# Products for VectorE, another order of the groups' pattern, and the seventh group routed through TensorE in a fused attention and expert kernel

## The chip, the cores and the metric

The kernel runs on one core of a Trainium2 chip. The metric is the device time of one execution in microseconds (us), as the median of several runs. The engines are TensorE (PE for its matmuls, PEld for its weight loads), VectorE (DVE), ScalarE (ACT), GpSimd (POOL) and SyncE (SP); each works through its own queue of instructions in order, and semaphores order the queues among each other. DMA transfers are issued from the queues of SP, ACT and POOL.

## The reference

Three stages follow one another: gated linear attention, a dense gated product, and a routed mixture of experts.

```python
# q, k, v, alpha: (4, 8, 768, 48)
for t in range(S):
    state = alpha[:, :, t, :, None] * state + einsum('bhd,bhe->bhde', k[:, :, t], v[:, :, t])
    y[:, :, t] = einsum('bhd,bhde->bhe', q[:, :, t], state)
x = y, as 3072 tokens of 384
x = (x @ w_a) * (x @ w_b) @ w_out          # 384 -> 1536 -> 384
logits = x @ w_gate + modality_bias[modality_id]   # 8 experts
e_idx = argmax(logits); gate_w = softmax(logits)[e_idx]
out[token] = gate_w * (relu(x @ w1[e_idx]) @ w2[e_idx])   # 384 -> 1024 -> 384
```

## The kernel before

The 3072 tokens are cut into eight groups (w = 0 to 7) of 384 tokens, two groups to a batch of the attention. A group has three chunks (c = 0 to 2) of 128 tokens and twelve features (f = 0 to 11), each a slice of 128 columns of `w_a` and `w_b` and 128 rows of `w_out`. Float32 operands of the dense stage are split in a high and a low part, and each product is three passes, so one feature of one group is 18 matmuls into `ab` (token m, L723), which ScalarE copies (`asb`, L728), VectorE multiplies (`g`, token g, L734), ScalarE rounds (`gh`, L736), VectorE subtracts (`gl`, token l, L741), and nine matmuls into `px` (token p, L693). TensorE runs m of one feature before p of the one before it.

A chunk of the attention goes through these tokens. 1, 2 and 3 each take the next piece of `prepare`: transpose and clip alpha, the scan `R` (L419) with its reciprocals, the scaled keys `kt` (L428), and then the scan `at` (L430), the transpose of q and the product `qt` (L432). S are the scores of `qt` and `kt` on TensorE (L444). M masks them into `sm`. V is three steps in one: `pads` copies a part of v on ScalarE (L471), `decay` multiplies the running `state` by `R` (L477), and `values` makes the output `y` from `state` (L492, L504) and from `sm` (L508, L513) on TensorE. H rounds `y` to `xh` on ScalarE (L525), X subtracts to `xl` on VectorE (L529); T turns the keys (L535) and copies them to `ktok` (L537); U makes the update `u` (L543) and D adds it to `state` (L559, L561). A class attribute `early` marks groups 0 and 1; `LATE` is 3.

Before the change, `qt` is on VectorE for groups 0 to 2 and on GpSimd for groups 3 to 7, and `decay` is on VectorE for group 0 and on GpSimd after it. The mask of groups 0 to 2 is a copy on ScalarE (L461) and a select on GpSimd (L462); that of groups 3 to 7 is one product on VectorE (L464).

The routing of a group (`route`, token R for its next piece) has two forms. With gate columns, 24 products with a running sum on VectorE (`junk`, L771, each with an 81 ns read of its sum) give the logits of three tiles of 128 tokens, two products to a piece. Without them, TensorE transposes `xr` (L779), ScalarE copies it (`xT`, L781) and TensorE multiplies by `wg_sb` (L785). Both go on with the argmax on VectorE (to `oh`, L806), the rank on TensorE (L815 to L819), the positions on VectorE, and three scattered writes from GpSimd's queue, `tab_d<-rec,posi` (L832), here called the puts. The table `tab_d` is filled beforehand by `clear_table` (L1241), a memset and a DMA from GpSimd's queue. W makes the gate columns, Z loads inputs, i ids, r one piece of a weight's conversion, and Y checks late inputs.

The order of DVE, PE, SP and ACT is written out by hand in two lists: SEQ, for the products of groups 0 and 1 with the attention of groups 1 and 2, and STEADY, run five times (w = 2 to 6, each four lines a chunk), which interleaves the products of group w with the attention of group w + 1 and the routing of group w - 1. A line of STEADY is one feature. Group 0's attention comes first (`first`). Group 7's products, group 6's routing and the table of the first expert slots stand in a later part (pool `m2`): one feature, five features beside the routing, two more, and then the last four beside `slots[0].split()`, which converts the first expert's weights (`w0he` and so on, L1067) as they land (`w1re`). The landing of `w1re` hangs on the puts of the routing, since the table of rows `rte` is read after them (L1019) and the slot's loads follow it. After that the expert slots run.

Of the kernel before, what the change touches and what calls it, by code (L numbers as in the profile page):

```python
# [20 lines left out]
P = 128  # L21
# [10 lines left out]
SEQ = (  # L32
# [16 lines left out]
)  # L49
# [14 lines left out]
)  # L64
WARM0, WARM1 = 7, (0, 3, 4, 0, 3, 0, 0, 0, 1)
ORDER0 = 3, 0, 1, 2, 1
MIX = 5, 2, 3
SPLIT = 4
# [5 lines left out]
def gla_moe_kernel(ctx, tc, q, k, v, alpha, w_a, w_b, w_out, modality_id, w_gate, modality_bias, w1, w2, out):  # L74
# [162 lines left out]
    def load_ids():  # L237
        idr = ap.tile([P, H * D], I32, tag="v", bufs=4, name="idr")[:NT, : 2 * P]
        nc.sync.dma_start(out=idr, in_=modality_id.rearrange("(t p) -> t p", p=P).bitcast(I32))
        mb = const.tile([P, 2, E], F32, name="mb")  # L240
        nc.sync.dma_start(out=mb, in_=modality_bias.rearrange("(o m) e -> o m e", o=1).broadcast_to([P, 2, E]))
        yield
        idf = ap.tile([NT, P], F32, tag="sm", bufs=3, name="idf")
# [11 lines left out]
        t0 = ap.tile([P, NT, E], F32, tag="sm", bufs=3, name="bias0")  # L255
# [67 lines left out]
    class Attention:  # L323
# [79 lines left out]
        def prepare(self, c):  # L403
# [27 lines left out]
            q0, qt = self.turned("q", c, 2)  # L431
            (nc.vector if self.w < LATE else nc.gpsimd).tensor_tensor(qt, q0, at, op=ALU.mult)  # L432
            self.ready[c] = Rp[:, :, 1:2], kt, qt
# [14 lines left out]
        def mask(self, c):  # L448
            self.sc[c] = []
            for g, pt in enumerate(self.pts.pop(c)):  # L450
# [8 lines left out]
                pv = pt.rearrange("p (h t) -> p h t", h=NPAIR)  # L459
                if self.w < LATE:  # L460
                    nc.scalar.activation(sm, pv, AF.Copy)  # L461
# [11 lines left out]
        def decay(self, c):  # L473

            if self.gc(c):
                R = self.ready[c][0]
                (nc.gpsimd if self.w else nc.vector).tensor_tensor(  # L477
                    state, state, R.broadcast_to([P, NPAIR, 2 * D]), op=ALU.mult
                )

        def values(self, c):
# [7 lines left out]
            if later:  # L489
                for kk in range(2):  # L490
                    for i in range(2):
                        mm = nc.tensor.matmul(  # L492
                            py[64 * i : 64 * i + 64, kk, :], state[:, 2 * kk + i, :64], qt[:, 2 * kk + i, :], start=(kk == 0), stop=False
                        )
                        if not (kk or i or self.w < LATE):
                            for n in ("mask", "pads"):
# [164 lines left out]
    def tokens(*groups):  # L661
# [14 lines left out]
        p = chain.from_iterable(a.prepare(c) for a in groups for c in range(CPW))  # L676
        names = dict(S=["scores"], M=["mask"], V=["pads", "decay", "values"], H=["high"], X=["low"], T=["keys"], U=["carry"], D=["add"])
        return {**{nm.upper(): turns(nm) for nm in "akq"}, **dict.fromkeys("123", p), **{t: each(*does) for t, does in names.items()}}

    def lazily(make):  # L680
        yield from make()

# [65 lines left out]
    def moe(w):  # L748
        for piece in products([(w, f) for f in range(NF)]):
            if piece in "le":  # L750
                yield

# [11 lines left out]
    def route(w, pool, puts, gate=None):  # L764
# [3 lines left out]
        for t in range(CPW):  # L768
# [7 lines left out]
            else:  # L776
                pt = ptile(f"xT{w}_{t}")
                for kk in range(KD):
                    nc.tensor.transpose(pt[:, kk * P : (kk + 1) * P], xr[w][t][:, kk * P : (kk + 1) * P], ident)  # L779
                xt = pool.tile([P, 512], F32, tag="sm", bufs=3, name=f"xT{w}_{t}")[:, :DM]  # L780
                nc.scalar.activation(xt, pt[:, :DM], AF.Copy)  # L781
# [458 lines left out]
    def clear_table():  # L1240
        fill = ap.tile([P, TAB // P * 2], F32, tag="sm", bufs=3, name="fill")  # L1241
        nc.gpsimd.memset(fill, BIG)
        nc.gpsimd.dma_start(out=tab_d.rearrange("(p r) c -> p (r c)", p=P), in_=fill)

    def turn_gate():

        pt = ptile("gateT")
        for kk in range(KD):
            nc.tensor.matmul(pt[:E, kk * P : (kk + 1) * P], wg_sb[:, kk, :], ident, start=True, stop=True)
        t = ap.tile([P, 512], F32, tag="sm", bufs=3, name="gateT")[:E, :DM]  # L1250
        nc.scalar.activation(t, pt[:E, :DM], AF.Copy)
        nc.scalar.dma_start(out=wgt_d[:, :], in_=t)

    def pipeline(y_d=None):
# [3 lines left out]
        with tc.tile_pool(name="att", bufs=1) as ap:  # L1258
# [19 lines left out]
            if y_d is None:  # L1278
                with tc.manual_schedule(engines={EN.DVE, EN.PE, EN.SP, EN.Activation}):
# [7 lines left out]
                    def second():  # L1287
# [4 lines left out]
                        load_weights(1, "ab")  # L1292
                        clear_table()

# [3 lines left out]
                    def gate_turn():  # L1298
                        turn_gate()
                        gate.append(gate_columns("gate", ap, 2, tag="cv", bufs=4))  # L1300
                        yield
# [19 lines left out]

                    extra = {"r": rest, "i": load_ids(), "W": gate_turn(), "Z": chain(then_load(then), then_load(nxt)), "R": lazily(lambda: route(0, ap, puts))}
                    todo = halves + [(w, f) for w in range(2, NW - 1) for f in range(NF)]
                    joint = products(todo)
# [29 lines left out]
                    for w in range(2, NW - 1):  # L1354
# [3 lines left out]
                        emit(STEADY, {**groups[w + 1], **kinds, "0": groups[w + 2]["1"]})  # L1358
                        assert not any(True for _ in chain(*(groups[w + 1][c] for c in "1SMVHXTUD"), *kinds.values()))
                    assert next(rest, None) is None  # L1360
                    assert next(joint) == "e"
            else:
# [10 lines left out]
        with tc.tile_pool(name="m2", bufs=2) as m2:  # L1373
            fold = small("fold", [P, TINY])
            nc.vector.tensor_reduce(fold, ident.rearrange("p (j c) -> p c j", c=TINY), axis=AX.X, op=ALU.add)
            last = moe(NW - 1)
            gate = gate_columns("last", m2, 4, tag="wr", bufs=6) if y_d is None else None
            run((islice(last, 1), 1))
            early = []
            run((islice(last, MIX[0]), 1), (behind(chain(route(NW - 2, m2, puts, gate), early_table(early))), 2))  # L1380
            slots = [Slot(f"e{i}", "e", i, 2, (NW - 1) * WIN) for i in range(NEARLY)]
# [173 lines left out]
```

## Time and profile before

| | us |
|---|---|
| median of 3 runs | 867.98 |
| lowest and highest of them | 867.70, 869.49 |
| the profiled execution, whole | 876.44 |
| its span, first to last instruction | 874.6 |
| busy: PE, DVE, ACT, POOL | 819.8, 674.0, 292.7, 206.0 |
| mean granted clock of TensorE | 0.987 |

The profiled execution is 8.46 us longer than the median of the runs, and 1.84 us longer than its own span. Rows of the trace give times from the span's start.

### The profile page before, as it was taken

The numbers are of one execution on the slowest core, as the hardware profiler recorded it, in microseconds if no ns is written. First come the engines' busy times: TensorE is split into PE (matmuls) and PEld (weight loads), VectorE is DVE, ScalarE is ACT, GpSimd is POOL, SyncE is SP. The second block draws the span as 40 slices with busy tenths as digits, with TensorE's granted clock in tenths as the row PEclk, the third lists the DMA queues.
The fourth block names the chain that finished last, engine by engine and source line by source line (L and its number), as shares of the span: only waits on it lengthen the run. The fifth ranks groups of instructions, "written<-read, shape, count | busy, mean of one in ns | idle before, by whom it ended". The sixth has DMA issues, their size and how long they took to land.

```text
span 874.6 us, 16828 instructions
## 1 busy us (share of the span) xinstructions
PE 819.8 (94%) x6193; PEld 771.2 (88%) x6193; DVE 674.0 (77%) x1495; ACT 292.7 (33%) x684; POOL 206.0 (24%) x283
## 2 busy tenths in 40 slices
PE   7778999999999998999999999899799999999995
PEld 6667998988998998998899899899699998998994
DVE  7878898659887987998998888774569876675641
ACT  2233442331222222221222222121555565564640
POOL 5221100102111012111111111102426554555421
PEclk9899999999999999999999999999899999999998
DMA  9988842716412410422422220030943988695900
GB/s 170 195 191 201 209 123 73 195 52 81 110 28 63 107 50 2 136 56 54 118 64 64 62 59 1 2 100 2 385 130 137 326 313 275 184 362 162 314 33 23
DMA packets 127089, 113.93 MB, mean 130 GB/s; under 512 B 55919, under 2 KB 105875, under 8 KB 126996
## 3 DMA queue, kind: packets, MB, share of 16 engines
q1 hardware_dynamic: 116260, 100.57, 42.2%
q0 software_dynamic: 4480, 10.99, 3.6%
q10 hardware_dynamic: 6256, 1.19, 1.1%
q8 instruction: 51, 0.84, 0.5%
q14 instruction: 42, 0.34, 0.1%
HBM read 101.87 MB, written 11.00 MB: 129 GB/s over the span
## 4 chain that ended last, share of the span: by engine, by line
PE 61%; DVE 21%; issue 6%; ACT 3%; POOL 3%; DMA 2%; another core or an unknown queue 2%; SPq 1%; DVEq 0%; POOLq 0%; ACTq 0%
PE ab L723 19%; PE px L693 9%; PE hl L1155 9%; PE pol L1103 8%; DVE R L419 3%; DVE at L430 2%; DVE g L734 2%; PE he L1155 2%; PE poe L1103 2%; PE s L444 2%; PE u L543 2%; DVE junk L771 2%; DVE kt L397 2%; DVE qt L397 1%
## 5 line engine op out<-in xcount | busy, mean ns | idle before, releaser
L723 PE MATMUL ab<-xh,pa 128*128 128x384 f32 x576 | 166.0, 342 | 7.9 <-ACT asb L728 5.5
L723 PE MATMUL ab<-xh,pb 128*128 128x384 f32 x576 | 163.4, 337 | 3.5 <-DVE pb L225 2.8
L693 PE MATMUL px<-po,gh 128*128 128x384 f32 x576 | 148.3, 342 | 0.4 <-DVE po L225 0.4
L723 PEld LDWEIGHTS ab<-xh,pa 128*128 128x128 f32 x576 | 106.4, 189 | 9.6 <-ACT asb L728 5.8
L723 PEld LDWEIGHTS ab<-xh,pb 128*128 128x128 f32 x576 | 106.1, 189 | 5.4 <-DVE pb L225 3.7
L736 ACT ACTIVATE gh<-g 128x384 fp32r<-128x384 f32 x96 | 50.3, 524 | 172.7 <-DVE g L734 171.4
L693 PEld LDWEIGHTS px<-po,gh 128*128 128x128 f32 x576 | 101.8, 188 | 3.8 <-issue 1.0
L723 PE MATMUL ab<-xl,pa 128*128 128x384 f32 x288 | 97.2, 337 | 0.3
L723 PE MATMUL ab<-xl,pb 128*128 128x384 f32 x288 | 96.8, 336 | 0.0
L728 ACT ACTIVATE asb<-ab 128x384 f32<-128x384 f32 x96 | 46.9, 489 | 145.5 <-PE ab L723 143.5
L693 PE MATMUL px<-po,gl 128*128 128x384 f32 x288 | 94.4, 337 | 0.3 <-DVE gl L741 0.3
L734 DVE TENSOR_TENSOR g<-ab,asb 128x384 f32<-128x384 f32 x96 | 53.2, 554 | 50.6 <-issue 26.7
L1160 DVE SCALAR_TENSOR_TENSOR hll<-hl,hhl 128x256 fp32r<-128x256 f32 x72 | 30.3, 421 | 54.1 <-ACT hhl L1158 50.4
L771 DVE SCALAR_TENSOR_TENSOR junk<-xr,gate 128x384 bf16<-128x384 f32 x96 | 65.2, 679 | 2.4
L477 POOL TENSOR_TENSOR state<-state,R 128x384 f32<-128x384 f32 x18 | 16.1, 895 | 203.1 <-DVE R L419 193.9
L741 DVE TENSOR_TENSOR gl<-g,gh 128x384 fp32r<-128x384 f32 x96 | 54.0, 563 | 9.7 <-ACT gh L736 9.7
L723 PEld LDWEIGHTS ab<-xl,pa 128*128 128x128 f32 x288 | 54.6, 190 | 0.8 <-DVE xl L529 0.8
L693 PEld LDWEIGHTS px<-po,gl 128*128 128x128 f32 x288 | 53.8, 188 | 1.0 <-DVE gl L741 1.0
L723 PEld LDWEIGHTS ab<-xl,pb 128*128 128x128 f32 x288 | 54.5, 189 | 0.0
L1158 ACT ACTIVATE hhl<-hl 128x256 fp32r<-128x256 f32 x72 | 27.7, 384 | 63.4 <-PE hl L1155 55.0
L832 POOL DMA_INDIRECT tab_d<-rec,posi x24 | 24.2, 1009 | 89.7 <-DVE base L829 50.1
L432 POOL TENSOR_TENSOR qt<-qt,at 128x512 f32<-128x512 f32 x15 | 20.3, 1355 | 89.3 <-DVE qt L397 89.3
(340 smaller groups left out, 1871.4 us busy)
## 6 DMA issues: line engine op xcount, KB each, us to landing
w1rl<-in_moe_w SPq DMA_DIRECT2D x18, 768.0 KB
w2rl<-in_moe_w SPq DMA_DIRECT2D x18, 768.0 KB
raw_a<-in_alpha SPq DMA_DIRECT2D x72, 96.0 KB
raw_k<-in_k SPq DMA_DIRECT2D x72, 96.0 KB
raw_q<-in_q SPq DMA_DIRECT2D x72, 96.0 KB
wo<-in_moe_w_out SPq DMA_DIRECT2D x6, 768.0 KB
w1re<-in_moe_w SPq DMA_DIRECT2D x6, 768.0 KB
w2re<-in_moe_w SPq DMA_DIRECT2D x6, 768.0 KB
```

The source lines that it names most:

```text
L397: nc.vector.transpose(t.rearrange("p a (r n) -> p a n r", n=self.TPP), self.raws.pop((nm, c)).rearrange("p a (n d) -> p a n d", d=D)[:, :, ...
L693: newest["mm"] = nc.tensor.matmul(px[w][t][:, :DM], a_, b_, start=(first and i == 0), stop=(last and i == 2))
L723: nc.tensor.matmul(pt[:, :WIN], a_, b_, start=(i == 0), stop=(i == 3 * KD - 1))
L728: nc.scalar.activation(asb, pt[:, :WIN], AF.Copy)
L734: nc.vector.tensor_tensor(g, pab[1][:, :WIN], asb, op=ALU.mult)
L736: newest["act"] = nc.scalar.activation(gh, g, AF.Copy)
L741: newest["gl"] = nc.vector.tensor_tensor(gl, g, gh, op=ALU.subtract)
L771: nc.vector.scalar_tensor_tensor(junk, xr[w][t], 1.0, gate[e], op0=ALU.mult, op1=ALU.mult, accum_out=L[:, t, e : e + 1])
L1103: newest["mm"] = nc.tensor.matmul(self.po[t][:, :DM], a_, b_, start=(f == 0 and i == 0), stop=(f == NF2 - 1 and i == 2))
L1155: nc.tensor.matmul(pt[:, :n], a_, b_, start=(i == 0), stop=(i == 3 * KD - 1))
L1158: nc.scalar.activation(gh[:, :n], pt[:, :n], AF.Relu)
L1160: nc.vector.scalar_tensor_tensor(gl[:, :n], pt[:, :n], 0.0, gh[:, :n], op0=ALU.max, op1=ALU.subtract)
```

## The change

The change has seven parts (paths with `y_d` given are not run). (a) `qt` and `decay` are on VectorE for all groups. (b) Group 2's mask is made on VectorE too, and the dependence of `values` on the mask and the pads holds from group 2 on. (c) `decay` and `pads` become a token of their own, E, which stands before M; V keeps only `values`; T stands before V; the next group's token 0 stands behind l. (d) In STEADY the sixth and twelfth pieces of the routing stand one line earlier or later than before, the rank (piece 14) one feature after the argmax (piece 13), and the last piece (positions and puts) behind D at the end. (e) `clear_table` leaves the start and becomes token C beside feature work of groups 0 and 1; `gate_turn` gives two pieces, the second at the end of SEQ. (f) Small tiles change their pool's tag from `sm` (3 buffers) to `cv` (4 buffers). (g) Group 7's first four features are interleaved with group 6's routing in a new list, FINAL, and that routing has no gate columns; the later part continues with one, two and then the remaining features, with `MIX = 1, 2, 2`.

```diff
-    "m p g 2 l i"
+    "m p g 2 l i C"
...
-    "m S W p g M l 1"
-    "m V H T p U g 2 X l D"
...
+    "m S W p g E M l 1"
+    "m T V H p U g 2 X l D"
...
 STEADY = (
     "m p g 1 l 2"
     "m p g 3 l R R"
-    "m S p g R l M R R"
-    "m V H T p U g 1 X l D"
-    "m p g 1 l 2"
+    "m S p g R l E M R R"
+    "m T V H p U g 1 X l D"
+    "m p g 1 l 2 R"
     "m p g 3 l R R"
-    "m S p g R l M R R"
-    "m V H T p U g 1 X l D Y"
-    "m p g 1 l 2"
-    "m p g 3 l R R Z Z"
-    "m S p g R l M R R"
-    "m V H T p U g 0 X l D Y"
+    "m S p g R l E M R R"
+    "m T V H p U g 1 X l D Y"
+    "m p g 1 l 2 R"
+    "m p g 3 l R Z Z"
+    "m S p g l E M R"
+    "m T V H p U g X l 0 D R Y"
+)
+FINAL = (
+    "m p g l"
+    "m p R g l R"
+    "m R p g R l R"
+    "m p R g l R"
 )
-MIX = 5, 2, 3
+MIX = 1, 2, 2
...
-            (nc.vector if self.w < LATE else nc.gpsimd).tensor_tensor(qt, q0, at, op=ALU.mult)
+            nc.vector.tensor_tensor(qt, q0, at, op=ALU.mult)
...
-                if self.w < LATE:
+                if self.early:
                     nc.scalar.activation(sm, pv, AF.Copy)
...
-                (nc.gpsimd if self.w else nc.vector).tensor_tensor(
-                    state, state, R.broadcast_to([P, NPAIR, 2 * D]), op=ALU.mult
-                )
+                nc.vector.tensor_tensor(state, state, R.broadcast_to([P, NPAIR, 2 * D]), op=ALU.mult)
...
-                        if not (kk or i or self.w < LATE):
+                        if not (kk or i or self.early):
                             for n in ("mask", "pads"):
...
-        names = dict(S=["scores"], M=["mask"], V=["pads", "decay", "values"], H=["high"], X=["low"], T=["keys"], U=["carry"], D=["add"])
+        names = dict(S=["scores"], M=["mask"], E=["decay", "pads"], V=["values"], H=["high"], X=["low"], T=["keys"], U=["carry"], D=["add"])
...
-                        clear_table()
...
                         turn_gate()
+                        yield
                         gate.append(gate_columns("gate", ap, 2, tag="cv", bufs=4))
...
-                    todo = halves + [(w, f) for w in range(2, NW - 1) for f in range(NF)]
+                    todo = halves + [(w, f) for w in range(2, NW) for f in range(NF)]
...
+                    late_route = route(NW - 2, ap, puts)
+                    emit(FINAL, {"R": late_route})
...
-            last = moe(NW - 1)
-            gate = gate_columns("last", m2, 4, tag="wr", bufs=6) if y_d is None else None
-            run((islice(last, 1), 1))
             early = []
-            run((islice(last, MIX[0]), 1), (behind(chain(route(NW - 2, m2, puts, gate), early_table(early))), 2))
+            if y_d is None:
+                last, routing, n = features(joint), late_route, MIX[0]
+            else:
+                last, routing, n = moe(NW - 1), route(NW - 2, m2, puts), NF // 2
+            run((islice(last, n), 1), (behind(chain(routing, early_table(early))), 2))
```

## Rows read from the trace of the kernel before

**Rows 1.** The page: busy time of each engine, and the chain's shares by engine.
```profile
PE 819.8 (94%) x6193; PEld 771.2 (88%) x6193; DVE 674.0 (77%) x1495; ACT 292.7 (33%) x684; POOL 206.0 (24%) x283
...
PE 61%; DVE 21%; issue 6%; ACT 3%; POOL 3%; DMA 2%; another core or an unknown queue 2%; SPq 1%; DVEq 0%; POOLq 0%; ACTq 0%
```

**Rows 2.** Stages: length; busy PE, PEld, DVE, ACT, POOL; granted clock; DMA share; GB/s.
```profile
20.00:45.00 25.00, 19.20 (x196) 15.87 (x196) 20.56 (x38) 6.84 (x14) 6.52 (x12) 0.86 0.97 191
...
272.30:418.10 145.80, 140.23 (x1089) 132.57 (x1089) 124.81 (x291) 34.06 (x80) 18.90 (x23) 1.00 0.27 70
...
602.50:633.70 31.20, 25.05 (x131) 24.08 (x130) 13.43 (x24) 12.60 (x29) 11.87 (x16) 0.89 0.75 266
```

**Rows 3.** The chain that ended last: start, length, what.
```profile
82.97 3.12 PE ab L723 x18
86.09 1.56 PE px L693 x9
...
600.12 5.99 DMA tab_d<-rec,posi
...
610.54 4.58 DMA w1re<-in_moe_w
...
617.53 6.01 PE ab L723 x18
```

**Rows 4.** Waits of all engines: us in total, times, the longest.
```profile
PE rank L815 <- DVE oh L806: 6.6, 6, 1.1
...
PE ab L723 <- ACT asb L728: 5.5, 1, 5.5
...
PE s L444 <- POOL qt L432: 4.9, 13, 1.1
```

**Rows 5.** Timeline of POOL, 5 to 90 us: start, us, instruction, idle before.
```profile
28.18 0.77 POOL L1243 DMA_DIRECT2D tab_d<-fill  x1 [5.97 <-issue]
...
88.26 1.70 POOL L705 DMA_DIRECT2D x_d<-xr  x3 [10.43 <-ACT xr L701]
```

**Rows 6.** Timeline of PE in the first group's attention.
```profile
29.94 0.64 PE L508 MATMUL y<-sm,v 128*32 128x128 f32 x2 [1.75 <-POOL sm L462]
```

**Rows 7.** Timeline of VectorE around two chunks of group 7.
```profile
532.48 1.28 DVE L464 TENSOR_TENSOR sm<-s,cmask 128x512 f32<-128x512 f32 x2
...
550.91 1.56 DVE L771 SCALAR_TENSOR_TENSOR junk<-xr,gate 128x384 bf16<-128x384 f32 x1
...
552.51 0.56 DVE L771 SCALAR_TENSOR_TENSOR junk<-xr,gate 128x384 bf16<-128x384 f32 x1
```

**Rows 8.** Timeline of PE at the first of these two chunks.
```profile
534.38 0.66 PE L492 MATMUL y<-qt,state 128*64 128x128 f32 x8
```

**Rows 9.** Timeline of all engines, last chunk of group 7.
```profile
559.28 1.02 POOL L832 DMA_INDIRECT tab_d<-rec,posi  x1 [7.23 <-DVE base L829]
...
560.93 0.62 PE L513 MATMUL y<-sm,vpad 128*32 128x128 f32 x16
...
563.60 0.49 ACT L525 ACTIVATE xh<-y 128x384 fp32r<-128x384 f32 x1 [4.55 <-remote]
```

**Rows 10.** Groups of VectorE's instructions by form: busy us, mean ns of one, idle before.
```profile
L771 DVE SCALAR_TENSOR_TENSOR junk<-xr,gate 128x384 bf16<-128x384 f32 x96 | 65.2, 679 | 2.4
L734 DVE TENSOR_TENSOR g<-ab,asb 128x384 f32<-128x384 f32 x96 | 53.2, 554 | 50.6 <-issue 26.7 <-PE ab L723 20.4 <-ACT asb L728 3.3
...
L424 DVE TENSOR_TENSOR starts<-starts,once 128x4 f32<-128x4 f32 x18 | 10.7, 593 | 0.6
...
L432 DVE TENSOR_TENSOR qt<-pq,at 128x512 f32<-128x512 f32 x6 | 4.2, 692 | 0.6
```

**Rows 11.** The same view, GpSimd's share.
```profile
L432 POOL TENSOR_TENSOR qt<-qt,at 128x512 f32<-128x512 f32 x15 | 20.3, 1355 | 89.3 <-DVE qt L397 89.3
```

**Rows 12.** Timeline of PE in the routing of group 0 on TensorE.
```profile
165.13 0.49 PE L779 MATMUL xT<-ident,xs 128*128 128x128 f32 x3
166.26 0.83 PE L785 MATMUL L<-wg_sb,xT 128*128 128x8 f32 x6 [0.64 <-ACT xT L781]
```

More of the change, by code (lines that the diff above doesn't have):

```diff
@@ L242, in load_ids @@
         yield
-        idf = ap.tile([NT, P], F32, tag="sm", bufs=3, name="idf")
+        idf = ap.tile([P, UNIT // 2], F32, tag="cv", bufs=4, name="idf")[:NT, :P]
         nc.vector.tensor_copy(idf, idr.rearrange("t (p w) -> t p w", w=2)[:, :, 0])
@@ L254, in load_ids @@
         nc.vector.tensor_scalar(is0, ids, 0.0, None, op0=ALU.is_equal)
-        t0 = ap.tile([P, NT, E], F32, tag="sm", bufs=3, name="bias0")
+        t0 = ap.tile([P, UNIT // 2], F32, tag="cv", bufs=4, name="bias0")[:, : NT * E].rearrange("p (t e) -> p t e", t=NT)
         bc = lambda t: t.unsqueeze(2).broadcast_to([P, NT, E])
@@ L676, in tokens, with features @@
         p = chain.from_iterable(a.prepare(c) for a in groups for c in range(CPW))
-        names = dict(S=["scores"], M=["mask"], V=["pads", "decay", "values"], H=["high"], X=["low"], T=["keys"], U=["carry"], D=["add"])
+        names = dict(S=["scores"], M=["mask"], E=["decay", "pads"], V=["values"], H=["high"], X=["low"], T=["keys"], U=["carry"], D=["add"])
         return {**{nm.upper(): turns(nm) for nm in "akq"}, **dict.fromkeys("123", p), **{t: each(*does) for t, does in names.items()}}
+    def features(pieces):
+        for piece in pieces:
+            if piece in "le":
+                yield
     def lazily(make):
-        yield from make()
+        yield from make() or ()
     def products(work_list):
@@ L748, in moe @@
     def moe(w):
-        for piece in products([(w, f) for f in range(NF)]):
-            if piece in "le":
-                yield
+        return features(products([(w, f) for f in range(NF)]))
     def gate_columns(name, pool, n, **tag):
@@ L779, in route @@
                     nc.tensor.transpose(pt[:, kk * P : (kk + 1) * P], xr[w][t][:, kk * P : (kk + 1) * P], ident)
-                xt = pool.tile([P, 512], F32, tag="sm", bufs=3, name=f"xT{w}_{t}")[:, :DM]
+                xt = (ap.tile([P, UNIT // 2], F32, tag="cv", bufs=4, name=f"xT{w}_{t}") if pool is ap else pool.tile([P, 512], F32, tag="sm", bufs=3, name=f"xT{w}_{t}"))[:, :DM]
                 nc.scalar.activation(xt, pt[:, :DM], AF.Copy)
@@ L1240, in clear_table @@
     def clear_table():
-        fill = ap.tile([P, TAB // P * 2], F32, tag="sm", bufs=3, name="fill")
+        fill = ap.tile([P, UNIT // 2], F32, tag="cv", bufs=4, name="fill")[:, : TAB // P * 2]
         nc.gpsimd.memset(fill, BIG)
@@ L1249, in turn_gate @@
             nc.tensor.matmul(pt[:E, kk * P : (kk + 1) * P], wg_sb[:, kk, :], ident, start=True, stop=True)
-        t = ap.tile([P, 512], F32, tag="sm", bufs=3, name="gateT")[:E, :DM]
+        t = ap.tile([P, UNIT // 2], F32, tag="cv", bufs=4, name="gateT")[:E, :DM]
         nc.scalar.activation(t, pt[:E, :DM], AF.Copy)
@@ L1299, in gate_turn @@
                         turn_gate()
+                        yield
                         gate.append(gate_columns("gate", ap, 2, tag="cv", bufs=4))
@@ L1320, in late_steps @@
                         yield
-                    extra = {"r": rest, "i": load_ids(), "W": gate_turn(), "Z": chain(then_load(then), then_load(nxt)), "R": lazily(lambda: route(0, ap, puts))}
-                    todo = halves + [(w, f) for w in range(2, NW - 1) for f in range(NF)]
+                    extra = {"r": rest, "i": load_ids(), "C": lazily(clear_table), "W": gate_turn(), "Z": chain(then_load(then), then_load(nxt)), "R": lazily(lambda: route(0, ap, puts))}
+                    todo = halves + [(w, f) for w in range(2, NW) for f in range(NF)]
                     joint = products(todo)
@@ L1358, in pipeline @@
                         emit(STEADY, {**groups[w + 1], **kinds, "0": groups[w + 2]["1"]})
-                        assert not any(True for _ in chain(*(groups[w + 1][c] for c in "1SMVHXTUD"), *kinds.values()))
+                        assert not any(True for _ in chain(*(groups[w + 1][c] for c in "1SMEVHXTUD"), *kinds.values()))
                     assert next(rest, None) is None
-                    assert next(joint) == "e"
+                    late_route = route(NW - 2, ap, puts)
+                    emit(FINAL, {"R": late_route})
             else:
```

16 rows, old and new, of the table SEQ are left out of this document.

## The prediction

> **What bounds the kernel now.** The page comes first. TensorE is busy for 94% of the span and has 61% of the chain that ended last; VectorE is busy for 77% and has 21% of the chain, GpSimd 3% [rows 1]. So time can be won only where TensorE stands still or runs slowly, and VectorE is the engine that most often makes it do so. The chain gives the unit: 18 matmuls of `ab` take 3.12 us and nine of `px` 1.56 us, so one feature is 4.68 us and nothing in the change shortens it [rows 3].
>
> The busy time by stage then tells where TensorE is not full [rows 2]. In the first attention (20 to 45 us) it is busy for 19.20 of 25.00 us at a granted clock of 0.86. In two steady groups (272.3 to 418.1 us) it is busy for 140.23 of 145.80 us at 1.00, so 5.6 us of two groups are idle; VectorE is busy for 124.81 us there, 86%. Around the first expert slot's weights (602.5 to 633.7 us) TensorE is busy for 25.05 of 31.20 us at 0.89. The waits name what ends these gaps [rows 4]: the rank matmuls wait for `oh` six times, 6.6 us; the scores wait for GpSimd's `qt` 13 times, 4.9 us; one wait of 5.5 us is `ab` behind ScalarE's copy. The timelines show the three places from near, and each is taken up below with its term.
>
> **The start: clear_table leaves it.** GpSimd stands 5.97 us before it issues the DMA that fills the table [rows 5]. Behind it in GpSimd's queue is the mask of chunk 2 of group 0, and TensorE's `y` of that chunk waits 1.75 us for the first half of it [rows 6]. In the timeline this `y`, its second half and the update end at about 35 us, with matmuls at half pace from 31 us. After the change the mask's select can start when ScalarE has copied the scores, up to 6 us earlier. TensorE can't win all of that: VectorE is busy for 20.56 of these 25 us and the DMA engines for 97% [rows 2], and they come next. Bounds: nothing, if VectorE or a transfer takes the place at once; 8 us, if the whole hold and 2 us of the slow pace go. I take the middle, −4.0 us.
>
> Where does the hold go? The next DMA that GpSimd issues is the store `x_d` at 88.26 us, before which GpSimd has been idle for 10.43 us; no mask of group 2 is behind it any more (b) and the decay has left too, so a hold of 6 us there delays nothing on the path [rows 5]. [...]
>
> **Group 2 (b, e).** Its mask needs two products on VectorE a chunk (1.28 us for both halves by rows 7) in place of a copy on ScalarE and a select on GpSimd; `gate_turn` moves. TensorE is fed there by products of groups 0 and 1, which don't wait. I take −0.5 us, between −2 and +2.
>
> **The rank (d), steady groups.** In each of the five groups the argmax chain of VectorE is issued just ahead of the rank, so TensorE waits for `oh`, 1.1 us at the longest [rows 4]. Five of the six waits are here (the sixth is group 0's routing, which stays): 6.6 − 1.1 = 5.5 us of idle time, and about 0.1 us at each restart, so −6.0 us. After the change a whole feature (4.68 us) lies between argmax and rank, and the argmax is ten small instructions of about 0.2 us. Bounds: −4 to −6.5.
>
> **The puts (d), steady groups.** In the last chunk of a group, `y` ends at 560.93 + 0.62 = 561.55 us, yet ScalarE starts `xh` only at 563.60 us, although it was idle for 4.55 us [rows 9]. In other chunks of this trace `xh` follows `y` within 0.1 us. What differs is that the three puts run from 559.28 us. TensorE's signal arrives 2.0 us late, and the next group's first `ab`, which needs this `xh`, stands for some 1.0 us, in each of the five groups (the timeline has 0.96 to 1.08). With the puts behind D, `xh` is through before they start. What the late signal hits then is the next feature's `asb` and `g`. These have 4.68 us less the four steps asb, g, gh and gl of about 0.55 us each [rows 10] before p needs `gl`, so 2.5 us of cover against 2.0. I take −4.5 us; bounds −5 and 0, the latter if the cover is too thin.
>
> **qt on VectorE (a).** GpSimd takes 1355 ns for `qt` [rows 11], VectorE 692 [rows 10]. The scores' wait was 4.9 us in 13 chunks [rows 4], and this is the most that can be won. Yet VectorE's own queue gets longer ahead of `qt` in two of three chunks, by the two moved products with a running sum, 1.2 us, and by 0.69 us of `qt`. I take half, −2.5 us; bounds −4.9 and +2.
>
> **decay and T (a, c).** The decay's 0.55 us (a product of 384 columns, as `g` [rows 10]) and `qt`'s 0.69 now stand on VectorE, ahead of the mask, and `y` waits for the mask. In group 7 the mask ends at 532.48 + 1.28 = 533.76 us and `y` starts at 534.38, so 0.62 us are free [rows 7, 8]; T ahead of V gives some 0.4 us more. Added ahead of the mask in two of three chunks is 0.55 + 0.69 + 1.2 = 2.4 us. What VectorE gets back: while GpSimd's `qt` runs, the product that VectorE has at that moment takes 1.56 us instead of 0.56 [rows 7], and beside the decay the four-column L424 takes 593 ns in the mean, where VectorE's other small products take some 170 [rows 10]. So a chunk gets back 1.0 + 0.4 = 1.4 us. Net 1.0 us later against 1.0 us free: I take +1.5 us over the 15 chunks (0.1 each); bounds 0 and +21 (the rival below). Over all, VectorE gains 15 × 1.0 + 18 × 0.4 = 22 us and the 24 products of the last routing (15 us), and takes on 15 × 0.69 + 18 × 0.55 + 6 × 0.68 = 24 us.
>
> [...]
>
> **The end (g).** Before, group 6's routing on VectorE is done when the last put is issued at 600.12 us; it is 5.99 us until it has landed, then come the table's read and the 4.58 us of `w1re` [rows 3]. It lands at 615.1 us, 51 us after the first `ab` of group 7. ScalarE's conversion waits for it with `asb` queued behind, so TensorE stands 5.5 us [rows 4], and the next 18 matmuls take 6.01 instead of 3.12 us [rows 3], at a granted clock of 0.89 in the stage [rows 2]. After: the routing is spread over four features and ends some 23 us after the first `ab`, where before the positions came at 33. So `w1re` lands near 41 us. Its conversion stands behind the eighth feature, at 4.0 + 8 × 4.68 = 41.4 us. The wait goes, barely: −5.5 us, −2.9 for the pace, −0.8 for `he` behind it. The price is the routing on TensorE: three transposes 0.49 us and six matmuls 0.83 us per tile by group 0's rows, with a wait for `xT` of 0.64 us [rows 12]; the transposes partly run under others, and I take 4.0 us for three tiles. Sum −5.2; I take −4.5 since the landing is so near, with bounds −6 and +4.
>
> (f) changes which buffers the small tiles take; I count nothing, since they are ten or so and far apart, at most a wait of 1 us.
>
> **Sum.** −4.0 − 0.5 − 6.0 − 4.5 − 2.5 + 1.5 − 4.5 = −20.5 us, from 876.4 to 855.9 us for a profiled execution. That execution lay 8.46 us above the median, so 847.5 us.
>
> **Rivals.** *VectorE falls behind (ends slower).* If the relief of 1.4 us a chunk doesn't come, because other stalls take its place, the mask is 2.4 us later against 1.0 us free: 1.4 us in each of 15 chunks, +21 us, and the scores' term is at its upper bound of +2. Then −20.5 + 2.5 + 2 − 1.5 + 21 = +3.5, so 871.5 us. It decides from 1.2 us a chunk on, (20.5 − 2.5 − 2 + 1.5) / 15. For it: VectorE is at 86% in this stage [rows 2]. Against: the two stalls stand in the rows, one per chunk. *The start gains nothing* (VectorE or the transfers are next): 851.5 us. For it: the 97% of the DMA engines. *The slot's weights still come late*: −5.5 − 2.9 fall away and the price stays, 856 us. For it: 41.1 against 41.4 us. *The puts hit the next group's features*: −4.5 falls away, 852 us. *More is won* (the start gives 8 us, the scores all): 841 us.
>
> **How the numbers follow.** Forecast (844 to 850 us) 0.50; more won 0.10; start without gain 0.12; weights late 0.10; puts 0.07; VectorE behind 0.09; something unseen of either sign 0.02. The range reaches from 840 to 860 us: it takes in all but the slower rival and the ends, some 0.15. Runs of this kernel differ by 0.2%, 1.7 us, which is taken as no change. Slower by more: 0.08, of the first rival most and some of the unseen; same 0.04; faster 0.88.
>
> **What would show it.** Right: no 6 us of "issue" at 22 us, and `y` of chunk 2 ends near 30 us; no wait of `rank` for `oh` in groups 3 to 7; `xh` of the last chunk within 0.1 us of `y`; no product with a running sum at 1.56 us, their mean near 560 ns instead of 679 [rows 10]; no 5.5 us wait behind `asb`. Wrong: a new wait of `y` for the mask (L464) over 0.3 us a chunk, or of the scores for VectorE's `qt` over 0.4, or `w1re` landing later than 41 us after group 7's first `ab`.

## The result and the profile after

The changed kernel took 848.13 us (median of 4 runs, 846.85 to 849.12) and the kernel before 868.74 us beside it. The ratio is 0.9762, with a 95% interval of 0.9743 to 0.9782: faster by 20.6 us. Forecast were 847.5 us, within 840 to 860.

The page shows where TensorE stands now. Engines first, then the chain by engine, as in [rows 1].

```profile
PE 813.2 (96%) x6220; PEld 771.7 (91%) x6220; DVE 656.2 (78%) x1489; ACT 291.4 (34%) x681; POOL 164.9 (20%) x244
...
PE 81%; DVE 11%; DMA 3%; issue 2%; SPq 1%; ACT 1%; POOLq 0%; POOL 0%; DVEq 0%; ACTq 0%
```

TensorE's share of the chain rose from 61 to 81%, VectorE's fell from 21 to 11%, although VectorE is as busy as before by share (78 against 77%). GpSimd's share went from 3% to 0. The next view has the windows of [rows 2] at the same times. The work in them isn't quite the same, since the changed kernel gets to each place earlier.

```profile
20.00:45.00 25.00, 21.59 (x222) 18.99 (x223) 22.48 (x45) 8.64 (x18) 4.06 (x8) 0.93 1.00 186
...
272.30:418.10 145.80, 144.35 (x1126) 137.40 (x1125) 129.19 (x320) 34.86 (x82) 6.47 (x12) 1.00 0.38 72
...
602.50:633.70 31.20, 30.97 (x232) 30.49 (x231) 21.60 (x63) 17.16 (x44) 10.10 (x10) 1.00 0.31 102
```

In the steady groups TensorE's idle time fell from 5.6 to 1.45 us of 145.8. At the start it is busy for 21.59 instead of 19.20 us of 25, at a granted clock of 0.93 instead of 0.86. The third window holds other work than before: group 7's products begin 21.6 us earlier. The place that compares with it is 580.9 to 612.1 us, and there TensorE is busy for all of the 31.2 us, at 1.00.

For a sum, the span is better cut where the work is the same in every kernel: at the first `ab` of group 2 and at that of group 7, found by counting 18 `ab` matmuls a feature. In the timeline of TensorE after the change these are:

```profile
189.93 0.42 PE L732 MATMUL ab<-xh,pa 128*128 128x384 f32 x1
...
542.54 0.33 PE L732 MATMUL ab<-xh,pa 128*128 128x384 f32 x1
```

Before they stood at 198.30 and 564.14. So in these two profiles the start went from 198.3 to 189.9 us, the steady groups from 365.8 to 352.6, and the end from 310.5 to 302.6. All kernels of the experiments are cut in this way below. The sum of these three, 29.5 us, is more than the timed 20.6, because the profiled execution of before (876.44 us) lay 7.7 us above the median timed beside the changed kernel (868.74), and that of after (846.85) 1.3 us below its own.

VectorE's groups by form answer [rows 10]:

```profile
L778 DVE SCALAR_TENSOR_TENSOR junk<-xr,gate 128x384 bf16<-128x384 f32 x96 | 53.3, 555 | 2.2
...
L438 DVE TENSOR_TENSOR qt<-qt,at 128x512 f32<-128x512 f32 x18 | 12.5, 692 | 0.6
L483 DVE TENSOR_TENSOR state<-state,R 128x384 f32<-128x384 f32 x20 | 11.2, 558 | 0.1
...
L430 DVE TENSOR_TENSOR starts<-starts,once 128x4 f32<-128x4 f32 x18 | 3.0, 167 | 0.6
```

The products with a running sum fell from 679 to 555 ns and the four-column product from 593 to 167, at the price of 15 more `qt` of 692 ns (3 of the 18 were on VectorE before) and 18 more decays of 558 ns (2 of the 20 were).

At the end of group 6's products, in the timeline of all engines, `xh` follows `y` as it should (compare [rows 9]):

```profile
540.32 0.62 PE L517 MATMUL y<-sm,vpad 128*32 128x128 f32 x16
...
541.01 0.49 ACT L529 ACTIVATE xh<-y 128x384 fp32r<-128x384 f32 x1 [2.86 <-PE y L517]
...
542.54 0.33 PE L732 MATMUL ab<-xh,pa 128*128 128x384 f32 x1
...
543.56 0.97 POOL L839 DMA_INDIRECT tab_d<-rec,posi  x1 [34.29 <-DVE posi L835]
```

`y` ends at 540.94 and `xh` starts at 541.01; the puts start 2.5 us later, when `xh` is through. And at the end ScalarE takes up `w0he` without a wait (its timeline):

```profile
581.35 0.49 ACT L737 ACTIVATE asb<-ab 128x384 f32<-128x384 f32 x1 [2.14 <-PE ab L732]
583.93 1.75 ACT L1074 ACTIVATE w0he<-w1re 128x384 fp32r<-128x384 f32 x4
```

That is 583.93 − 542.54 = 41.4 us after the first `ab` of group 7, where the prediction put it. The trace has no landing of `w1re` itself here; it was issued at 578.96 us. The chain there runs through TensorE alone, feature by feature; the 6.01 us of [rows 3] are 3.23 and 3.12:

```profile
579.58 3.23 PE ab L732 x18
582.81 1.56 PE px L702 x9
584.37 3.12 PE ab L732 x18
```

### The profile page after: what moved, and what is told of

Read it like the earlier page. It is cut to its first block, busy times and chain, and to the rows that moved or that the text cites. A ratio compares the mean times of both kernels' runs of the same rounds, so it can differ in the third digit from the quotient of the medians.

```text
span 845.1 us, 16804 instructions
## 1 busy us (share of the span) xinstructions
PE 813.2 (96%) x6220; PEld 771.7 (91%) x6220; DVE 656.2 (78%) x1489; ACT 291.4 (34%) x681; POOL 164.9 (20%) x244
## 4 chain that ended last, share of the span: by engine, by line
PE 81%; DVE 11%; DMA 3%; issue 2%; SPq 1%; ACT 1%; POOLq 0%; POOL 0%; DVEq 0%; ACTq 0%
PE ab L732 30%; PE px L702 16%; PE hl L1162 9%; PE pol L1110 9%; PE s L450 3%; PE he L1162 2%; PE poe L1110 2%; PE u L547 2%; DVE R L425 1%; PE y L496 1%; PE y L512 1%; DMA wb<-in_moe_w_b 1%; PE y L517 1%; DMA wa<-in_moe_w_a 1%; DVE at L436 1%
## 5 line engine op out<-in xcount | busy, mean ns | idle before, releaser
L702 PE MATMUL px<-po,gh 128*128 128x384 f32 x576 | 150.3, 343 | 0.3 <-DVE po L231 0.3
L702 PE MATMUL px<-po,gl 128*128 128x384 f32 x288 | 96.4, 337 | 0.8 <-DVE gl L750 0.8
L417 POOL MEMSET at<- 128x4 f32 x24 | 2.5, 105 | 324.4 <-DVE qt L438 324.4
L778 DVE SCALAR_TENSOR_TENSOR junk<-xr,gate 128x384 bf16<-128x384 f32 x96 | 53.3, 555 | 2.2
L450 PEld LDWEIGHTS s<-qt,kt 64*128 64x128 f32 x384 | 24.5, 191 | 9.7 <-PE ab L732 7.1
## 6 DMA issues: line engine op xcount, KB each, us to landing
wo<-in_moe_w_out SPq DMA_DIRECT2D x6, 768.0 KB, 10.5
```

The source lines that it names most:

```text
L450: nc.tensor.matmul(pts[g][:, i * P : (i + 1) * P], kt[o : o + 64, i, :], qt[o : o + 64, i, :], start=True, stop=True)
L702: newest["mm"] = nc.tensor.matmul(px[w][t][:, :DM], a_, b_, start=(first and i == 0), stop=(last and i == 2))
L778: nc.vector.scalar_tensor_tensor(junk, xr[w][t], 1.0, gate[e], op0=ALU.mult, op1=ALU.mult, accum_out=L[:, t, e : e + 1])
```

## The experiments

All times of the table are in us. "Before" is the kernel before, timed beside each kernel on the same chip. Chips differ (the median of before was 873.2 on one and 867.8 to 868.7 on the others), so ratios that were taken on different chips are less comparable than their intervals say. The three stages are read from each profile as above. The steady one repeats itself: 365.84 in both profiles of before, and 352.53 to 352.69 in the six kernels that don't change it.

```
kernel         median  before  ratio to before, 95%       start   steady   end
before           -       -                                198.30  365.84  310.46
before_again   872.87  873.17  (one run)                  196.59  365.84  308.67
after          848.13  868.74  0.9762 (0.9743 to 0.9782)  189.93  352.62  302.56
after_again    848.97  868.64  0.9771 (0.9749 to 0.9792)  192.61  352.61  303.57
u_clear        852.25  873.17  0.9752 (0.9734 to 0.9770)  193.74  352.69  304.57
u_clear_sp     850.49  868.64  0.9794 (0.9773 to 0.9814)  190.17  352.61  304.92
u_clear_warm   857.85  867.78  (one run)                  200.16  352.53  303.31
u_pool         865.87  873.17  0.9907 (0.9891 to 0.9924)  192.66  368.27  304.27
b_pool         881.66  868.64  1.0157 (1.0097 to 1.0217)  200.72  372.37  308.31
u_late_e       881.36  867.78  1.0171 (1.0136 to 1.0206)  197.82  377.97  302.80
u_keys         852.44  867.78  0.9829 (0.9801 to 0.9857)  190.57  355.00  302.73
u_order        857.55  873.17  0.9819 (0.9802 to 0.9836)  189.71  361.65  304.04
u_last         860.04  868.64  0.9911 (0.9885 to 0.9936)  191.43  352.54  313.33
better         845.62  867.78  0.9745 (0.9721 to 0.9768)  190.42  349.59  302.89
```

**Two kernels measured again.** `before_again` is the kernel before.

> The kernel before, profiled once more, because its profiled execution lay 8.46 us above the median of its runs. Theory A: the 8.5 us lie in one place, the start, where GpSimd stood 5.97 us ahead of the table's DMA; then this execution has a span near 866, and the first ab of group 0 starts at 30 us or earlier instead of 36.8. Theory B: they are spread over the span; then the first ab stays at 36 to 37 us and the span may be anywhere between 866 and 875. The steady groups (72.9 us each) are the same in both.

Theory A is out, and theory B held but for 0.4 us: the first `ab` stands at 35.58 us and the hold is there (GpSimd stood 6.56 us ahead of the table's DMA), so it is no accident of one execution. None of the 8.46 us lies in the steady groups, which agree to 0.01 us. Where they do lie isn't shown, since this profile comes from a chip on which before is slower (its span is 871.1 us, the median there 873.2).

`after_again` is the changed kernel.

> The changed kernel once more, beside the kernel before on the same chip, as the measure for the other runs, since chips differ: before took 868.7 us beside the first timing and 873.2 beside the experiments so far. Theory: the ratio to before is the 0.976 of the first timing on any chip. Rival: it hangs on the chip, and then lies outside 0.974 to 0.978.

The theory held: 0.9771 against 0.9762. The start differs by 2.7 us between its two profiles, so a start stage is known to some 3 us only.

**The table at the start.** `u_clear` puts the filling of the table back.

```diff
-    "m p g 2 l i C"
+    "m p g 2 l i"
...
                         load_weights(1, "ab")
+                        clear_table()
```

> The changed kernel with the filling of the table back at the start (its tile back in the tag sm). Theory A: the hold of GpSimd ahead of that DMA comes back, with 6 us, and delays the mask of chunk 2 of group 0; the time rises from 848 by 4 to 9 us, to 852 to 857. Rival: the start was gained by the order of decay, pads and keys, and the hold is hidden; then 848 within 1 us, and the first ab stays near 30 us.

GpSimd's timeline of this kernel has the hold back, and TensorE's has the wait for it:

```profile
27.95 0.78 POOL L1250 DMA_DIRECT2D tab_d<-fill  x1 [6.47 <-issue]
```

```profile
30.08 1.45 PE L512 MATMUL y<-sm,v 128*32 128x128 f32 x13 [2.62 <-POOL sm L468]
```

The first `ab` comes at 36.39 instead of 30.41 us. Yet at group 2 only 1.1 to 3.8 us of the 6 are left (193.74 against 192.61 and 189.93). A part of the difference is that the changed kernel, being early, waits 1.88 us at 34.46 us for the second half of the first weights (`pb`), which `u_clear` doesn't. The ratio alone, 0.9752, shows no loss, but it was taken on the chip on which before is slow. `u_order` was timed on the same chip: it is 5.3 us slower in time and 8.96 slower in the steady stage, so outside this stage `u_clear` is the slower one, by some 3.7 us. Theory A's range begins at 4; what was measured is 1 to 4.

`u_clear_sp` issues the same DMA from SyncE's queue.

```diff
-        nc.gpsimd.dma_start(out=tab_d.rearrange("(p r) c -> p (r c)", p=P), in_=fill)
+        nc.sync.dma_start(out=tab_d.rearrange("(p r) c -> p (r c)", p=P), in_=fill)
```

> The changed kernel with the table filled at the start again, but by a DMA from SyncE's queue instead of GpSimd's. Theory A (the hold belongs to GpSimd's queue): no 6 us ahead of the mask, the first ab of group 0 starts at 30 to 31 us as in the changed kernel, and the time is that of the changed kernel within 1.5 us. Rival (the hold belongs to the transfers, which are busy for 97% there): the mask or a weight comes late all the same, and the first ab starts at 34 us or later.

The first `ab` is at 31.01 us and the start is 190.17, as theory A has it; the time is 1.5 us above that of `after_again` on the same chip, at the edge of its range. But this doesn't show that the hold belongs to GpSimd's queue. SyncE's timeline has the table's DMA only at 39.41 us, behind the loads written ahead of it, and so not in the stretch of the hold; and in that stretch SyncE, too, took 3.85 us to issue one load:

```profile
21.69 3.85 SPq L370 DMA_DIRECT2D raw_q<-in_q  x1
...
39.41 0.40 SPq L1250 DMA_DIRECT2D tab_d<-fill  x1
```

What is shown is that the mask isn't late when no DMA stands ahead of it in GpSimd's queue (its select starts at 24.04 us here, at 28.75 in `u_clear`). Whether the hold is GpSimd's own or that of the loaded transfers stays open. `u_clear_warm` has a small DMA as the first of GpSimd's queue.

```diff
                 nc.gpsimd.memset(starts, 0.0)
+                nc.gpsimd.dma_start(out=dram.tile([P, 4], F32, name="warm_d")[:, :], in_=starts[:, :4])
```

> The changed kernel with the table filled at the start from GpSimd's queue, and ahead of it, as the first DMA of that queue, one of 16 bytes a partition to a spare buffer. Theory A (the hold is paid by the first DMA of GpSimd's queue): the 6 us stand ahead of the small DMA at 5 us, and the table's DMA near 22 us has none. Theory B (the hold belongs to this place and load): the table's DMA is held by 6 us all the same.

GpSimd's timeline:

```profile
6.57 0.78 POOL L1269 DMA_DIRECT2D warm_d<-starts  x1
...
33.83 0.59 POOL L1250 DMA_DIRECT2D tab_d<-fill  x1 [3.76 <-issue]
```

The first DMA is issued at once, and the second, the table's, is held by 3.76 us. Theory A is out, and theory B holds in kind; the table's DMA also stands some 6 us later here than in `u_clear`. This kernel's time says nothing about the hold, since VectorE waited 7.83 us to write `starts`, which the small DMA was reading.

**qt and decay.** `u_pool` takes both back to GpSimd in the changed kernel.

```diff
-            nc.vector.tensor_tensor(qt, q0, at, op=ALU.mult)
+            (nc.vector if self.w < LATE else nc.gpsimd).tensor_tensor(qt, q0, at, op=ALU.mult)
...
-                nc.vector.tensor_tensor(state, state, R.broadcast_to([P, NPAIR, 2 * D]), op=ALU.mult)
+                (nc.gpsimd if self.w else nc.vector).tensor_tensor(state, state, R.broadcast_to([P, NPAIR, 2 * D]), op=ALU.mult)
```

> The changed kernel with qt of groups 3 to 7 and decay of groups 1 to 7 back on GpSimd; the order of all the rest stays. Theory A (GpSimd stood in VectorE's way as much as it helped): the mean of the products with a running sum goes back from 555 to about 680 ns, the scores wait some 0.45 us in 13 of 15 chunks again, and the time is 850 to 853. Rival (VectorE has become the tighter engine): with 2 us a chunk taken off it the time falls below 847.

The direction is theory A's, the size is not: the steady groups take 368.27 instead of 352.61 us, 15.7 us more. The waits name it:

```profile
PEld s L450 <- POOL qt L438: 21.8, 14, 1.7
PE s L450 <- POOL qt L438: 17.3, 14, 1.3
```

Before, the same wait was 4.9 us [rows 4]. It is larger here because a moved piece of the routing stands ahead of `qt` on VectorE, so GpSimd, whose `qt` takes 1343 ns here where VectorE's takes 692 in the changed kernel, gets q later: in the timelines VectorE has turned q 3.15 us after a feature's first `ab`, in two of three chunks, where it was 2.08 us in the kernel before. The piece was not moved back by itself.

`b_pool` is the other side: the kernel before with `qt` and `decay` on VectorE and nothing else.

```diff
-            (nc.vector if self.w < LATE else nc.gpsimd).tensor_tensor(qt, q0, at, op=ALU.mult)
+            nc.vector.tensor_tensor(qt, q0, at, op=ALU.mult)
...
-                (nc.gpsimd if self.w else nc.vector).tensor_tensor(
+                nc.vector.tensor_tensor(
```

> The kernel before with qt and decay on VectorE for all groups and nothing else changed, so the decay stands behind the mask on VectorE. Theory A (as forecast for this part): the scores' wait of 4.9 us goes, the products with a running sum fall from 679 to 555 ns in the mean, and the time falls by 2 to 5 us. Rival (VectorE falls behind): y waits for mask and decay by 0.5 us or more a chunk, and the time is unchanged or rises by up to 8 us.

The rival, and worse than it was priced: 1.0157 (1.0097 to 1.0217), 13 us slower. The relief came (the products with a running sum take 555 ns), and the scores' wait for `qt` went, but the waits have a new row:

```profile
PE y L492 <- DVE state L477: 24.1, 13, 2.7
```

VectorE's timeline of one chunk shows how the decay is late: it is written behind the mask and four products of the routing, and `y` of TensorE starts only at 249.55.

```profile
245.37 1.28 DVE L464 TENSOR_TENSOR sm<-s,cmask 128x512 f32<-128x512 f32 x2
246.57 0.55 DVE L771 SCALAR_TENSOR_TENSOR junk<-xs,gate 128x384 bf16<-128x384 f32 x1
...
248.85 0.55 DVE L477 TENSOR_TENSOR state<-state,R 128x384 f32<-128x384 f32 x1
```

Counted by features, the steady groups of `b_pool` lose 20.9 us at their fourth and eighth feature, where this `y` stands, and win 14.4 us at others, against before. A part of what they win is unforeseen: at the end of each group `xh` follows `y` at once, although the puts stand where they stood in the kernel before, the first of them 2.3 us ahead of the end of `y` in both (compare [rows 9]). The timeline of all engines, last chunk of group 7:

```profile
569.18 1.10 POOL L832 DMA_INDIRECT tab_d<-rec,posi  x1 [34.33 <-DVE posi L828]
...
570.86 0.62 PE L513 MATMUL y<-sm,vpad 128*32 128x128 f32 x16
...
571.54 0.49 ACT L525 ACTIVATE xh<-y 128x384 fp32r<-128x384 f32 x1 [2.57 <-PE y L513]
```

It is so in all five groups (0.07 us from `y` to `xh`, against 2.0 in the kernel before). So the puts beside `y` are not enough to make `xh` late.

**The place of decay, pads and keys.** `u_late_e` leaves decay on VectorE and puts E behind M and T, right ahead of V, in every line of both lists.

```diff
-    "m S p g R l E M R R"
-    "m T V H p U g 1 X l D"
+    "m S p g R l M R R"
+    "m T E V H p U g 1 X l D"
```

> The changed kernel with E (decay and pads) behind M and T, right ahead of V, where these steps were before. Theory A: with decay on VectorE behind the mask, y waits some 2 us for it in two of three chunks, as when decay alone was put on VectorE; the time rises by 12 to 20 us over the changed kernel. Rival: T ahead of V covers the decay, and the time rises by less than 4 us.

Theory A, and more: 1.0171, with 25.4 us in the steady groups and 5 to 8 at the start. The main wait is that of `b_pool`; the third row is the pads, which moved along with the decay, and the two weren't taken apart:

```profile
PE y L496 <- DVE state L483: 24.2, 13, 2.4
PEld y L496 <- issue: 21.7, 12, 2.7
PEld y L496 <- ACT vpad L477: 8.8, 6, 1.9
```

`u_keys` puts T behind V again.

```diff
-    "m T V H p U g 1 X l D"
+    "m V H T p U g 1 X l D"
```

> The changed kernel with T behind V again, in both lists. Theory A: y starts 0.4 us earlier and waits for the mask in some chunks; u waits for ktok again, 1.4 and 1.1 us at the start and 1.1 in two later groups; the time rises by 2 to 6 us. Rival: T's place costs and gains nothing beyond 1 us, since the features beside it cover it.

The steady groups take 2.4 us more, and `y` waits for the mask, which T ahead of it had covered:

```profile
PE y L496 <- DVE sm L470: 2.8, 7, 0.5
```

So theory A holds for the steady groups with the lower end of its size; two waits of `u` came back in the timeline of TensorE, only at the start (1.72 us, which the profile puts down to `qt`, and 0.75 us for `ktok`), and 190.57 is within the spread of the start.

**Rank and puts.** `u_order` restores the routing's pieces in STEADY.

```diff
-    "m p g 1 l 2 R"
-    "m p g 3 l R Z Z"
-    "m S p g l E M R"
-    "m T V H p U g X l 0 D R Y"
+    "m p g 1 l 2"
+    "m p g 3 l R R Z Z"
+    "m S p g R l E M R R"
+    "m T V H p U g X l 0 D Y"
```

> The changed kernel with the routing's pieces in STEADY where they stood before: rank right behind the argmax, puts ahead of the last chunk's y. Theory A: the rank waits 1.3 to 1.5 us again in each of five groups, and the last xh of a group comes 2 us late again, which costs 1.0 to 1.3 us; together 12 to 13 us, so 860 to 861. Rival: with the keys ahead of y and qt on VectorE one of the two waits is hidden, and the time is 853 to 856.

9.0 us in the steady groups, between the two. Both waits are back, the rank's with 0.71 us in each of five groups, where the kernel before had 1.12 (the sixth, of 1.5 us, is group 0's and stands in the changed kernel too). The first row is ScalarE's idle time (`remote` is a releaser that the profile can't name); the delay in it, from the end of `y` to `xh`, is 2.1 to 2.5 us:

```profile
ACT xh L529 <- remote: 22.3, 5, 5.3
...
PE rank L822 <- DVE oh L813: 5.0, 6, 1.5
...
PE ab L732 <- ACT xh L529: 3.7, 3, 1.3
```

**The end.** `u_last` gives group 6's routing back to VectorE in the later part, with `MIX = 5, 2, 3`.

```diff
-                    late_route = route(NW - 2, ap, puts)
-                    emit(FINAL, {"R": late_route})
+                    assert next(joint) == "e"
...
+            last = moe(NW - 1)
+            gate = gate_columns("last", m2, 4, tag="wr", bufs=6) if y_d is None else None
```

> The changed kernel with its end as before: group 6 routed by gate columns on VectorE beside group 7's features in the later part, MIX 5, 2, 3. Theory A: w1re lands some 10 us later against group 7's features again, ab waits 5.5 us and the next 18 matmuls run at half pace; less the 3.6 us that the transposes and logits take on TensorE, the time rises by 5 to 8 us against the changed kernel. Rival: with the table and the puts earlier the wait is gone anyway, and the time falls by 3 us since TensorE is spared the routing.

Theory A in kind: the end takes 313.33 instead of 302.56 and 303.57 us. The waits have `asb` behind the weights again, and one that the sum didn't have: VectorE waits 9.7 us for the gate columns to land (3.6 in the kernel before), and `ab` for a `g` behind the products that need them. So this end isn't quite that of the kernel before, and its 10 us are more than the 5 to 8 us by which the end itself differs between before and after.

```profile
PE ab L732 <- ACT asb L737: 5.0, 1, 5.0
...
PE ab L732 <- DVE g L743: 3.7, 3, 2.5
```

**A loss in the changed kernel.** Counting features, groups 5 and 6 each lose time at their second and third one in the changed kernel (0.84 + 0.61, and 0.81 us less 0.17, against before). VectorE's timeline at the start of group 5's products, and TensorE's:

```profile
405.00 0.74 DVE L327 TENSOR_REDUCE amax<-late 128x2 f32<-128x576 f32 x1
...
408.23 0.55 DVE L750 TENSOR_TENSOR gl<-g,gh 128x384 fp32r<-128x384 f32 x1
```

```profile
408.84 0.45 PE L702 MATMUL px<-po,gl 128*128 128x384 f32 x1 [0.39 <-DVE gl L750]
...
413.99 0.38 PE L450 MATMUL s<-qt,kt 64*128 64x128 f32 x2 [0.51 <-DVE qt L438]
```

The check of the late inputs stands between the positions and `g`, so `gl` and then `qt` are late. `better` moves Y by one feature.

```diff
-    "m S p g l E M R"
-    "m T V H p U g X l 0 D R Y"
+    "m S p g l E M R Y"
+    "m T V H p U g X l 0 D R"
```

> The changed kernel with the check of the late inputs (Y, four reductions of 0.74 us on VectorE) moved from the end of a group, behind D and the last piece of the routing, to one feature earlier, behind M and the rank. Theory A: at the end of groups 5 and 6 the positions, the puts and this check come together on VectorE, gl and the scores of the next group come late by 0.6 to 0.85 us each, and this goes: 2 to 3 us, a ratio to before of 0.972 to 0.974. Rival: the loss there comes from the inputs that the puts hold up (raw_k lands late), and the time stays at the changed kernel's 0.976.

The steady groups take 349.59 us, 3.0 less, all of it at these features (0.85 and 0.61 us in group 5, 0.81 and 0.60 in group 6). The inputs' DMAs are still issued slowly there (four `raw_k` take SyncE 4.76 us, 7.02 in the changed kernel, whose next four, at 431.55 us, take 1.74), and VectorE's timeline of the changed kernel has no gap of more than 0.1 us from 402.9 to 413 us, so it waited for no input there. So it was VectorE's order. The ratio of 0.9745 lies just above theory A's 0.972 to 0.974, and its interval overlaps that of the changed kernel: the 3.0 us are shown by the stage, not by the times.

## Why the prediction was right

The forecast time and its sign held, and so did the mechanism in the main: the waits that the prediction names went. How it shares the gain out among the parts of the change didn't hold, and that 847.5 came within 0.6 us of 848.13 is partly luck. The forecast has −4.5 us for the start (with group 2), −11.5 for the steady groups and −4.5 for the end; the profiles have −4.0 to −8.4, −13.2 and −5 to −8, so the steady groups and the end won more than their terms. Of the signs of being wrong one came in part: the scores wait for VectorE's `qt` six times, 2.1 us in all and up to 0.5. No wait of `y` for VectorE's mask came.

*Start, −4.0.* The stage went from 198.30 and 196.59 to 189.93 and 192.61, −4.0 to −8.4. The table's own share is 1 to 4 us by `u_clear`, so the term's cause was right and its size at the upper end. What the prediction didn't count is E: with decay and pads late the start is 5 to 8 us longer (`u_late_e`).

*Where the hold goes.* The prediction prices a hold of 6 us at the store `x_d` as costing nothing; that it would move there was the author's estimate, and no run shows it. In the changed kernel `x_d` is the first DMA of GpSimd's queue and stood only for `xr`, 10.22 us, as this part of the timeline shows; nor was the table held where C puts it, with 0.30 us before it. In `u_clear_warm`, too, the first DMA of this queue was issued without a hold, at 6.57 us.

```profile
79.37 1.88 POOL L714 DMA_DIRECT2D x_d<-xr  x3 [10.22 <-ACT xr L710]
...
119.91 0.54 POOL L1250 DMA_DIRECT2D tab_d<-fill  x1 [0.30 <-POOL fill L1249]
```

*Rank, −6.0, and puts, −4.5.* Counted by features, the changed kernel gains 1.38 to 1.47 us at the eleventh feature of each group, where the rank stands, 7.2 us in all, and 1.2 to 1.6 us a group at its end, some 6.5 us, of which groups 5 and 6 give back 2 us. Not all of this is due to the new places. `b_pool`, which leaves the routing where it stood, gains 0.8 us at each eleventh feature (the rank's wait falls from 1.12 to 0.71 us, and the scores' wait goes) and 1.1 to 1.4 us at each end. With (a) made, the rank's new place is worth 0.61 to 0.67 us a group by `u_order`, 3.3 us in all and not 6.0; with the puts' it is 9.0, against 10.5 forecast. The puts' new place does away with the late `xh`, but the prediction's reason for it, that the signal is late because the puts run, is incomplete: in `b_pool` they run and `xh` is on time. What else it takes stays open.

*qt, −2.5, decay and T, +1.5.* This is the weakest step, though the sum hides it. The terms were taken one by one and added: −1.0 us for (a) with the new places of E and T. They don't add. In the steady groups (a) without the new order costs 6.5 us (`b_pool`, 13 in all), the new order without (a) costs 2.4 (`u_pool` against before), and both together gain 13.2; in the changed order (a) is worth 15.7 us. The reason is named in the prediction, but on the wrong side: the decay isn't dear by its 0.56 us ahead of the mask, it is dear by standing behind the mask and the routing's products, and E ahead of M is what avoids that. The relief was as forecast (555 and 167 ns); in `u_pool`, with `qt` and `decay` back on GpSimd, the two means are 637 and 560 ns, and what makes VectorE slower beside GpSimd was not shown. The first rival, VectorE late for `y`, is real and comes to its price or more as soon as the decay stays where it was: 20.9 us of lost features in `b_pool` and 25.4 in `u_late_e` (the pads are in this one), against the 21 worked out. It comes about in another way than the one priced, since the relief did come. What decided against it was the order of (c), and not the relief.

*End, −4.5.* The stage went from 310.46 and 308.67 to 302.56 and 303.57, −5 to −8; the conversion of the weights began at 41.4 us as forecast and without a wait, and group 7's first four features lost 3.3 us to the routing on TensorE where 4.0 were taken.

*Group 2, −0.5,* was not measured by itself.

## What to carry to other kernels

Where queues are in a written order, the engine of an operation and its place in the queue are one decision: the same move of two products cost 6.5 us in the old order and gained 15.7 in the new. Price such parts together, by asking for each instruction what stands ahead of it on its new engine when its consumer comes. And cut profiles at the same piece of work: here the steady stage repeated itself to 0.2 us where whole runs differed by 5 between chips, so that 3 us could be seen which the times could not show.

## What the runs showed of the hardware

The table's DMA from GpSimd's queue was held 5.97, 6.56, 6.47, 5.5 and 3.76 us in the five profiles that have it at the start (before, `before_again`, `u_clear`, `b_pool`, `u_clear_warm`), and not at 119.91 us in the changed kernel, with 0.30 us before it. It isn't the price of the queue's first DMA, which was issued at once at 6.57 us in `u_clear_warm`. It was seen only at the start, where two other things stand out: VectorE works without a gap of more than 0.05 us in the holds of before, `before_again`, `u_clear` and `u_clear_warm`; and SyncE takes 3.73 to 4.03 us to issue the load of q at 21.69 to 21.87 us, with the table's DMA or without it (4.03 in before, 3.92 in `u_clear`, 3.85 in `u_clear_sp`, 3.73 in the changed kernel), where the next load of q takes 0.60 to 0.65 in before, `u_clear_sp` and the changed kernel. No run separates these, and the cause stays open.

`xh` started 2.0 to 2.5 us after the `y` that it waits for in the last chunk of five groups, in the kernel before and in `u_order`, while three scattered writes were being issued from GpSimd's queue; elsewhere in the kernel before it started 0.05 to 0.07 us after, and once 0.36 (at 26.44 us). It was not late in `b_pool`, with the writes in the same place, so the writes alone don't make it, and what does stays open.
